# Seven products of a two-layer block in another order, with layer-two blocks between them, four buffers for early heads, weight conversions queued behind them, and one subtraction on VectorE

## The chip, the core and the metric

The kernel runs on one core of a Trainium2 chip. The core has a matrix engine (TensorE, PE in the profile; its weight loads are PEld), three engines for elementwise work (VectorE or DVE, ScalarE or ACT, GpSimd or POOL), and a queue (SyncE, SP) that issues every DMA here. Each engine works its own queue in order; semaphores hold an instruction until what it reads is written and what it overwrites has been read. The metric is device time in microseconds; less is better.

## The reference

Windowed attention with a linear position bias, then a two-layer block with a piecewise-quadratic gate:

```python
# q, k, v: 8 batches x 8 heads x 576 tokens x 64, f32 (q and k times 8)
scores = scale * q @ k.T - slope[h] * abs(i - j)
scores = where((i - j >= 0) & (i - j < 128), scores, -1e9)
attn = exp(scores - max) / (sum + 1e-9)
x = (attn @ v), heads side by side          # 4608 tokens x 512
h = x @ w_in                                # 512 x 2048
g = where(h >= 1, h, where(h <= -1, 0, (h + 1)**2 / 4))
out = g @ w_out                             # 2048 x 512
```

Inputs are drawn at random; `w_in` and `w_out` reach the chip as 64-bit floats.

## The kernel before

**Tiling.** The 36 blocks of 128 tokens form ten chunks (`SIZES`, L54): 2 blocks, eight times 4, and 2. Chunk c is worked in two steps: its attention (8 heads, in four pairs) fills `xn[c]`, the transposed activations; then a *sweep* over the 16 column groups of the hidden layer takes them through both layers. While the sweep of chunk c runs, the attention of chunk c+1 is emitted between its steps (`emit_attention`, L478; the attention's pieces stand in the list `segments`, L458, and run an eighth of a sweep ahead). A scheduler puts each engine's instructions in order from the program's order, taken as priority, and from a simulated time line.

**Precision.** From chunk 2 on a f32 operand is split in two parts, a rounded one and the rest, as fast `fp32r` numbers, and a product is made of two or three fast matmuls. Chunks below `LIGHT = 2` (L62) use plain f32 matmuls in the attention instead (one matmul, two instructions of the engine, no split). So `prepare_q` (L232), `prepare_k` (L252) and `prepare_v` (L263) make split copies only from chunk 2 on.

**One head.** `scores` (L273): PE writes scores, VectorE folds the window into one 128x128 tile per block (L302, L304), ScalarE takes the exponential (L306), the row sums are inverted (L308, L309) and scale `z`, on VectorE in light chunks (L311), on ScalarE otherwise (L314). `weights_t` (L316), a head later: PE transposes `z` (L323), ScalarE copies the result to `lu` (L326), VectorE makes its rest (L328), and GpSimd makes two triangular halves of it (L336, L338) for the two key blocks that a query block sees. `values` (L341), two heads later: PE multiplies by v (L363), and the result goes to `xn` (L366 in light chunks; L368 and L369 otherwise). `lu` has one buffer, `z` two. In the light chunks a matmul of `values` covers up to two query blocks.

**First sweep.** `first_sweep` (L587) takes plain f32 weights. They are made on the chip from the 64-bit words: `fetch_raw` (L127) loads a 0.5 MB tile into one of six buffers, and `convert` (L132) takes two ScalarE and two VectorE operations (L140, L143, L144, L147). There are 32 tiles; `weights_upto` (L485) emits conversions during the attention of chunk 0 and during the first sweep.

**The other sweeps.** A group g of a full sweep has seven products (`PRODUCTS`, L29), a Strassen-like scheme in which 2x2 quarters of weights (A11 ... S4) meet quarters of tokens (B11 ... T4). Each product is six fast matmuls of 256 columns (L411), into one of two accumulator banks, `hA` and `hB`. In `prod` (L533) the bank of product n is A for n = 0, 2, 3, 4 and B for 1, 5, 6. Products 2, 3 and 4 go on accumulating onto what A holds, so ScalarE takes a snapshot first (L539), and VectorE adds snapshots to results of B (L542, L547, L549). L544 copies the last state of A. Each finished tile `h` goes through `nonlinear` (L416): VectorE clamps (L418), ScalarE squares (L419), VectorE takes the maximum (L424), ScalarE rounds it to `gh` (L430), and GpSimd subtracts to make the rest `gl` (L431).

**Layer two.** `layer2` (L434) is a block of three fast matmuls of 512 columns (L445 to L447) from `gh` and `gl` into one of four accumulators. The eight blocks of group g are emitted between the products of group g+1 (`later`, L519): 1, 1, 2, 1, 1, 2 after products 1 to 6. The eight blocks of the last group go into the next sweep, one after each step.

**Weights and tokens.** In sweep 1 `build` (L170) splits each weight quarter and stores it to DRAM; later sweeps fetch it, ten ahead (`AHEAD`, L506), into a ring of ten buffers. `tokens_ready` (L391) lists, by product number, which token quarters of the next chunk may be split (`split_x`, L382) or combined (`combine`, L388) during the last group of a sweep, once the old quarter in the same buffer has had its last use. T2 is made after B22 has been split and overwritten.

Of the kernel before, what the change touches and what calls it, by code (L numbers as in the profile page):

```python
# [28 lines left out]
PRODUCTS = (("A11", "B11"), ("A12", "B21"), ("S2", "T2"), ("S1", "T1"), ("S4", "B22"), ("S3", "T3"), ("A22", "T4"))  # L29
# [5 lines left out]
def windowed_attention_then_ffn(  # L35
# [26 lines left out]
    LIGHT = 2  # L62
# [14 lines left out]
    def bank(c, name):  # L77
        turn[0] += 1
        if c < LIGHT and turn[0] % 2:
            return ps_acc.tile([P, 4 * P], F32, name=name, tag="acc1")  # L80
        return ps_a.tile([P, 4 * P], F32, name=name, tag="ps_a")
# [104 lines left out]
    pair, head, xn = {}, {}, {}  # L186
# [86 lines left out]
    def scores(m, blks):  # L273
# [4 lines left out]
        if m not in head:  # L278
            head[m] = dict(z=ap.tile([P, 4, P], F32, name=f"z_{m}", tag="z", bufs=2),
                           nmax=ap.tile([P, 4], F32, name=f"nmax_{m}", tag="nmax", bufs=2),  # L280
                           sum=ap.tile([P, 4], F32, name=f"sum_{m}", tag="sum", bufs=2),
                           rc=ap.tile([P, 4], F32, name=f"rc_{m}", tag="rc", bufs=2))
# [24 lines left out]
        if blks[-1] == nb - 1:  # L307
            V.tensor_scalar(rc[:, :nb], sm[:, :nb], 1.0e-9, None, ALU.add)  # L308
            V.reciprocal(rc[:, :nb], rc[:, :nb])  # L309
            if c < LIGHT:  # L310
                V.tensor_tensor(z[:, :nb], z[:, :nb], rc[:, :nb].unsqueeze(2).broadcast_to([P, nb, P]), ALU.mult)  # L311
# [4 lines left out]
    def weights_t(m):  # L316
# [3 lines left out]
        lu = head[m]["lu"] = ap.tile([P, 2, 8, P], F32R, name=f"lu_{m}", tag="lu")  # L320
# [3 lines left out]
        ns = 1 if c < LIGHT else 2  # L324
        kind = F32 if c < LIGHT else F32R
        S.copy(lu[:, 0, 1:2 * nb:2].bitcast(kind), pt)  # L326
        if ns == 2:
            V.tensor_tensor(lu[:, 1, 1:2 * nb:2], pt, lu[:, 0, 1:2 * nb:2].bitcast(F32), ALU.subtract)  # L328
        if ns == 2 and nb < 4:
            flat = lu[:, :, :2 * nb]  # L330
            odd, even, n = [flat[:, s, 1::2] for s in range(2)], [flat[:, s, 0::2] for s in range(2)], nb
        else:
            flat = lu.rearrange("p s i w -> p (s i) w")[:, :2 * nb * ns]
            odd, even, n = [flat[:, 1::2]], [flat[:, 0::2]], nb * ns
        for a, b in zip(odd, even):
            G.affine_select(out=b.bitcast(kind), in_=a.bitcast(F32), pattern=[[0, n], [-1, P]],  # L336
                            base=0, channel_multiplier=1, compare_op=ALU.is_gt, fill=0.0)
            G.affine_select(out=a.bitcast(kind), in_=a.bitcast(F32), pattern=[[0, n], [1, P]],  # L338
                            base=0, channel_multiplier=-1, compare_op=ALU.is_ge, fill=0.0)

    def values(m):  # L341
# [13 lines left out]
        todo = [(i, s) for i in range(first, nb) for s in range(1 if c < LIGHT else 2)]  # L355
# [346 lines left out]
```

## Time and profile before

| what | us |
|---|---|
| median of three runs (lowest, highest) | 1143.41 (1140.61, 1147.15) |
| the profiled execution | 1146.27 |
| its span, first to last instruction | 1144.2 |
| first row of the output issued, sweep of chunk 0 | 150.7 |
| the same for chunk 1 | 301.3 |
| the same for chunk 7 | 999.5 |
| last row of the output issued | 1140.1 |

The profile is of one execution. Rows of the views have the line of the kernel, the engine, the operation, the tile written and the tiles read, a count, the busy time in us and the mean in ns of one; behind the second bar stands the idle time of the engine just before them and what ended it. Matmuls overlap in the pipeline, so PE's busy time says less than the distance between the starts of its matmuls. The granted clock is the share of TensorE's full clock.

### The profile page before, as it was taken

Reading aid. Unit: us, or ns where it says so; the run is one execution under the profiler, and the core shown is the slowest. Engines: PE = TensorE matmul, PEld = TensorE weight load, DVE = VectorE, ACT = ScalarE, POOL = GpSimd, SP = SyncE. Lnnn points to the kernel's source line nnn. Section 1 sums busy time; section 2 is a strip of 40 time slices with the busy share of each in tenths; the row PEclk is TensorE's granted clock in tenths of the full one; section 3 lists DMA queues with packets and bytes.
Section 4 is the critical chain, followed back from the end, with each engine's and each line's share of the span. In section 5 each row is a group of like instructions: output and inputs, shape, how many; then the busy total and the mean of one; then the engine's idle time right before and its main releaser. Section 6 shows DMA issues by size and latency. Waiting matters only on the chain.

```text
span 1144.2 us, 19669 instructions
## 1 busy us (share of the span) xinstructions
PE 1046.4 (91%) x6320; PEld 919.0 (80%) x6320; DVE 802.8 (70%) x1934; ACT 744.7 (65%) x1894; POOL 404.7 (35%) x370
## 2 busy tenths in 40 slices
PE   5689978799899999998999899989999989999998
PEld 4567767688788878887989798868888879888897
DVE  6796579899777786777767866775669866864232
ACT  6895368677776676666767666755667765665332
POOL 3211135463333344333434243423333433433222
PEclk7699979999999999998999899989999999999999
DMA  9862135445666566656656666645565745565562
GB/s 327 303 230 67 45 109 172 158 150 179 207 183 186 159 203 181 183 157 190 180 167 191 176 179 182 175 140 170 175 175 177 208 151 169 154 198 155 169 202 74
DMA packets 102342, 199.01 MB, mean 174 GB/s; under 512 B 11361, under 2 KB 14945, under 8 KB 102241
## 3 DMA queue, kind: packets, MB, share of 16 engines
q1 hardware_dynamic: 102240, 197.77, 56.8%
q8 instruction: 51, 0.84, 0.3%
q14 instruction: 51, 0.41, 0.1%
HBM read 171.51 MB, written 26.21 MB: 173 GB/s over the span
## 4 chain that ended last, share of the span: by engine, by line
PE 67%; DVE 15%; ACT 10%; issue 4%; DMA 2%; POOL 1%; SPq 1%; DVEq 0%; ACTq 0%; POOLq 0%
PE hA L411 12%; PE acc L445 10%; PE acc L446 10%; PE acc L447 9%; PE hB L411 8%; PE x L363 5%; PE acc L442 2%; PE p L323 2%; PE h L596 2%; PE h L411 2%; PE s L299 2%; ACT m L419 2%; DVE ql L250 2%; PE s L300 2%; DVE h L424 1%
## 5 line engine op out<-in xcount | busy, mean ns | idle before, releaser
L431 POOL TENSOR_TENSOR gl<-h,gh 128x512 fp32r<-128x512 f32 x128 | 192.1, 1507 | 263.8 <-ACT gh L430 251.2
L445 PE MATMUL acc<-wo,gh 128*128 128x512 f32 x544 | 218.3, 401 | 5.6 <-ACT gh L430 5.6
L336 POOL TENSOR_SCALAR_AFFINE_SELECT lu<-lu 128x1024 fp32r<-128x1024 f32 (+3 forms) x88 | 85.2, 968 | 379.6 <-DVE lu L328 248.3
L446 PE MATMUL acc<-wo,gh 128*128 128x512 f32 x544 | 215.7, 397 | 0.0
L447 PE MATMUL acc<-wo,gl 128*128 128x512 f32 x544 | 163.3, 399 | 0.0
L306 ACT ACTIVATE z<-z,nmax 128x128 f32<-128x128 f32 x288 | 113.5, 395 | 58.8 <-DVE nmax L304 57.7
L419 ACT ACTIVATE m<-m,half 128x512 f32<-128x512 f32 (+1 forms) x160 | 107.8, 679 | 56.7 <-DVE m L418 53.3
L418 DVE TENSOR_SCALAR m<-h 128x512 f32<-128x512 f32 (+1 forms) x160 | 72.3, 458 | 78.6 <-ACT h L544 54.0
L445 PEld LDWEIGHTS acc<-wo,gh 128*128 128x128 f32 x544 | 104.1, 191 | 27.6 <-ACT gh L430 7.9
L424 DVE TENSOR_TENSOR h<-h,m 128x512 f32<-128x512 f32 x128 | 115.1, 903 | 14.5 <-ACT m L419 14.3
L446 PEld LDWEIGHTS acc<-wo,gh 128*128 128x128 f32 x544 | 104.2, 192 | 19.2
L411 PE MATMUL hA<-x_T,w_S 128*128 128x256 f32 x672 | 104.0, 289 | 14.3 <-ACT s L539 12.5
L411 PEld LDWEIGHTS hA<-x_T,w_S 128*128 128x128 f32 x672 | 91.9, 191 | 23.5 <-ACT s L539 16.9
L314 ACT ACTIVATE z<-z,rc 128x128 f32<-128x128 f32 x240 | 77.9, 392 | 50.3 <-DVE rc L309 49.7
L447 PEld LDWEIGHTS acc<-wo,gl 128*128 128x128 f32 x544 | 94.9, 190 | 12.7 <-POOL gl L431 0.2
L302 DVE COPY_PREDICATED s<-older,s 128x256 f32<-128x256 uint32 x144 | 60.8, 422 | 61.5 <-PE s L300 46.9
L539 ACT COPY s<-hA 128x256 f32<-128x256 f32 x192 | 69.7, 363 | 48.0 <-PE hA L411 47.4
L430 ACT CAST gh<-h 128x512 fp32r<-128x512 f32 x128 | 79.2, 621 | 25.3 <-DVE h L424 25.0
L363 PEld LDWEIGHTS x<-lu,vs 128*128 128x128 f32 x608 | 83.7, 192 | 12.3 <-POOL lu L338 4.8
L363 PE MATMUL x<-lu,vs 128*128 128x128 f32 (+1 forms) x608 | 84.8, 275 | 6.4 <-POOL lu L338 3.9
L338 POOL TENSOR_SCALAR_AFFINE_SELECT lu<-lu 128x1024 fp32r<-128x1024 f32 (+3 forms) x88 | 88.2, 1002 | 4.9 <-DVE lu L328 1.1
L323 PE MATMUL p<-ident,z 128*128 128x128 f32 x288 | 58.1, 292 | 19.9 <-ACT z L314 9.0
(116 smaller groups left out, 2217.9 us busy)
## 6 DMA issues: line engine op xcount, KB each, us to landing
w_S<-d_S SPq DMA_DIRECT2D x224, 256.0 KB, 3.0
w_A<-d_A SPq DMA_DIRECT2D x200, 256.0 KB, 2.8
kr<-in_k_dram SPq DMA_DIRECT2D x61, 320.0 KB, 4.9
vn<-in_v_dram SPq DMA_DIRECT2D x32, 320.0 KB, 3.5
out_dram<-o SPq DMA_DIRECT2D x36, 256.0 KB, 2.7
qr<-in_q_dram SPq DMA_DIRECT2D x33, 256.0 KB, 4.7
raw<-in_moe_w_in_dram SPq DMA_DIRECT2D x16, 512.0 KB, 5.5
raw<-in_moe_w_out_dram SPq DMA_DIRECT2D x16, 512.0 KB, 5.1
```

Source lines behind the costliest of these rows:

```text
L306: S.activation(z[:, i], z[:, i], AF.Exp, bias=nmax[:, i:i + 1], scale=-1.0, accum_out=sm[:, i:i + 1])
L323: T.transpose(pt[:, i], z[:, i], ident)
L336: G.affine_select(out=b.bitcast(kind), in_=a.bitcast(F32), pattern=[[0, n], [-1, P]], base=0, channel_multiplier=1, compare_op=ALU.is_gt, ...
L338: G.affine_select(out=a.bitcast(kind), in_=a.bitcast(F32), pattern=[[0, n], [1, P]], base=0, channel_multiplier=-1, compare_op=ALU.is_ge, ...
L363: T.matmul(px[:, q0 * P:q1 * P], st, mv.rearrange("p a w -> p (a w)"), start=(w == 0), stop=(w == len(todo) - 1), skip_group_check=True)
L411: T.matmul(o, w[:, a, kb], x[:, b, kb], start=start and n == 0, stop=stop and n == len(todo) - 1, skip_group_check=True)
L419: S.activation(m, m, AF.Square, bias=half[:, 0:1], scale=0.5)
L424: V.tensor_tensor(f, h, m, ALU.max)
L431: G.tensor_tensor(gl, f, gh.bitcast(F32), ALU.subtract)
L445: T.matmul(a, gh[:, ts], w[:, 0], start=first, stop=False)
L446: T.matmul(a, gh[:, ts], w[:, 1], start=False, stop=False)
L447: T.matmul(a, gl[:, ts], w[:, 0], start=False, stop=last)
```

## The change

- **Order of the products.** (S3, T3) moves from place 5 to place 3; (S1, T1) and (S4, B22) move one back. The banks become A B A B A A B, the snapshots are taken after products 0, 2 and 4, and the sum with B's first part (L547 before) is made after product 4. The token quarters become ready in the new order: T3 after product 3, T1 after 4, B22 and T2 after 5.
- **Urgent evacuation.** Snapshots, sums and the copy of A are emitted at a priority 200 places ahead.
- **Layer two.** Blocks go through one list `waiting` for all sweeps; `second` emits the oldest, and only while more than four are left. Places: 2, 0, 2, 2, 1, 1 after products 1 to 6.
- **gl on VectorE** instead of GpSimd (L431).
- **LIGHT = 3.** Chunk 2's attention is plain f32 as well. The alternate use of an accumulator bank for attention stays with chunks 0 and 1 (`FIRST = 2`).
- **Light heads.** The two triangular halves become two tiles, `own` and `old`; a matmul of `values` covers one query block, and each pair of query and key block has its own.
- **Early heads.** For chunk 0 `z` and the two halves take buffers of later tiles, four each; `weights_t` comes two heads and `values` three heads behind `scores` for chunk 0 (one and two as before from chunk 1 on).
- **Conversions behind.** Eight conversions are emitted during chunk 0's attention, each queued behind a head's copy and scaling on the same engines; the others come two for each step of the first sweep, queued behind its square and maximum, and the first ten builds behind its last four steps.

```diff
-PRODUCTS = (("A11", "B11"), ("A12", "B21"), ("S2", "T2"), ("S1", "T1"), ("S4", "B22"), ("S3", "T3"), ("A22", "T4"))
+PRODUCTS = (("A11", "B11"), ("A12", "B21"), ("S2", "T2"), ("S3", "T3"), ("S1", "T1"), ("S4", "B22"), ("A22", "T4"))
...
-    LIGHT = 2
+    LIGHT = 3
+    FIRST = 2
...
-            head[m] = dict(z=ap.tile([P, 4, P], F32, name=f"z_{m}", tag="z", bufs=2),
+            head[m] = dict(z=fp.tile([P, 2, P], F32, name=f"z_{m}", tag="sw", bufs=4) if c == 0 else
+                           ap.tile([P, 4, P], F32, name=f"z_{m}", tag="z", bufs=2),
...
+        if c < LIGHT:
+            if c < FIRST:
+                own, old = [fp.tile([P, 4, P], F32, name=f"{x}_{m}", tag=x, bufs=4)[:, :nb] for x in ("gh", "gl")]
+            else:
+                both = ap.tile([P, 2, 8, P], F32, name=f"lu_{m}", tag="lu")
+                own, old = both[:, 0, :nb], both[:, 1, :nb]
+            head[m]["lu"] = own, old
+            copied = S.copy(own, pt)
+            G.affine_select(out=old, in_=own, pattern=[[0, nb], [-1, P]],
+                            base=0, channel_multiplier=1, compare_op=ALU.is_gt, fill=0.0)
+            G.affine_select(out=own, in_=own, pattern=[[0, nb], [1, P]],
+                            base=0, channel_multiplier=-1, compare_op=ALU.is_ge, fill=0.0)
+            turned[m] = [copied.ins, head[m]["scaled"].ins]
+            return
...
-        todo = [(i, s) for i in range(first, nb) for s in range(1 if c < LIGHT else 2)]
+        todo = [(i, s) for i in range(first, nb) for s in range(2)]
+        if c < LIGHT:
+            todo = [(i, s) for i, s in todo if 0 <= i + s < nb]
...
-            4: [lambda: split_x(c, "B22", "B22"),
+            3: [lambda: split_x(c, "T3", "B12")],
+            4: [lambda: split_x(c, "T1", "B11")],
+            5: [lambda: split_x(c, "B22", "B22"),
                 lambda: combine(c, "B22", "B22", "B11"),
                 lambda: split_x(c, "T2", "B22"),
-                lambda: split_x(c, "T1", "B11"),
                 lambda: combine(c, "B21", "B21", "B22")],
-            5: [lambda: split_x(c, "T3", "B12")],
...
-        G.tensor_tensor(gl, f, gh.bitcast(F32), ALU.subtract)
+        V.tensor_tensor(gl, f, gh.bitcast(F32), ALU.subtract)
...
+        d1, d2 = (2, 3) if m < H else (1, 2)
+        work.append((m + d2, 0, m, [lambda m=m: values(m)]))
+        work.append((m + d1, 2, m, [lambda m=m: weights_t(m)]))
...
+    def behind(instructions, f):
+        with ExitStack() as stack:
+            for i in instructions:
+                stack.enter_context(tc.issue_after(i))
+            f()
...
-                    o = st["A" if n in (0, 2, 3, 4) else "B"]
-                    product(o, use(c, g, w), xs[c, x], start=n in (0, 1, 5), stop=True)
-                    if n in (0, 2, 3):
-                        s = st[n] = fp.tile([P, 2 * P], F32, name=f"s{n}_{c}_{g}", tag=f"s{n}", bufs=1)
-                        S.copy(s, o)
+                    o = st["A" if n in (0, 2, 4, 5) else "B"]
                     f1, f2 = st["h"]
-                    if n == 1:
-                        V.tensor_tensor(f1[:, :2 * P], o, st[0], ALU.add)
-                    if n == 4:
-                        S.copy(f1[:, 2 * P:], o)
+                    product(o, use(c, g, w), xs[c, x], start=n in (0, 1, 3), stop=True)
+                    with tc.high_priority(offset=URGENT):
+                        if n in (0, 2, 4):
+                            s = st[n] = fp.tile([P, 2 * P], F32, name=f"s{n}_{c}_{g}", tag=f"s{n}", bufs=1)
+                            S.copy(s, o)
+                        if n == 1:
+                            V.tensor_tensor(f1[:, :2 * P], o, st[0], ALU.add)
+                        if n == 4:
+                            V.tensor_tensor(f2[:, 2 * P:], st["B"], st[4], ALU.add)
+                        if n == 5:
+                            S.copy(f1[:, 2 * P:], o)
+                        if n == 6:
+                            V.tensor_tensor(f2[:, :2 * P], o, st[2], ALU.add)
+                    if n == 5:
                         nonlinear(c, g, f1, 4 * P)
...
-                for n, fill in ((2, 1), (3, 2), (4, 1), (5, 1), (6, 2)):
+                for n, fill in ((1, 2), (2, 0), (3, 2), (4, 2), (5, 1), (6, 1)):
...
+    KEEP = 4
+
+    def second():
+        if len(waiting) > KEEP:
+            waiting.pop(0)()
...
+                    weights_upto(EARLY + 2 * n + 2, squared[fc])
+                    if n >= NFC - 4:
+                        behind(squared[fc], lambda: operands_upto(3 * (n - NFC + 4) + 1))
...
+    EARLY = 8
+    while at[0] < ready[1]:
+        emit_attention(at[0] + 1)
+        if turned and converted[0] < EARLY:
+            last = max(turned)
+            if last + 1 > converted[0]:
+                weights_upto(converted[0] + 1, turned[last])
+    weights_upto(EARLY, turned[H - 1])
```

More of the change, by code (lines that the diff above doesn't have):

```diff
@@ L78, in bank @@
         turn[0] += 1
-        if c < LIGHT and turn[0] % 2:
+        if c < FIRST and turn[0] % 2:
             return ps_acc.tile([P, 4 * P], F32, name=name, tag="acc1")
@@ L182, in fetch @@
         return t
-    pair, head, xn = {}, {}, {}
+    pair, head, xn, turned = {}, {}, {}, {}
     lo_rows = [slice(0, D), slice(D, P)]
@@ new lines, in weights_t @@
+        lu = head[m]["lu"] = ap.tile([P, 2, 8, P], F32R, name=f"lu_{m}", tag="lu")
+        S.copy(lu[:, 0, 1:2 * nb:2], pt)
+        V.tensor_tensor(lu[:, 1, 1:2 * nb:2], pt, lu[:, 0, 1:2 * nb:2].bitcast(F32), ALU.subtract)
+        if nb < 4:
+            odd, even, n = [lu[:, s, 1:2 * nb:2] for s in range(2)], [lu[:, s, 0:2 * nb:2] for s in range(2)], nb
+        else:
+            flat = lu.rearrange("p s i w -> p (s i) w")
+            odd, even, n = [flat[:, 1::2]], [flat[:, 0::2]], 2 * nb
@@ L418, in nonlinear @@
         V.tensor_scalar(m, h, 1.0, -1.0, ALU.min, ALU.max)
-        S.activation(m, m, AF.Square, bias=half[:, 0:1], scale=0.5)
+        a = S.activation(m, m, AF.Square, bias=half[:, 0:1], scale=0.5)
         if SIZES[c] == 2:
@@ L516, in sweep_steps @@
     def sweep_steps(c):
-        steps, before = [], []
-        def later(k):
-            take, before[:] = before[:k], before[k:]
-            return take
+        steps = []
         for g in range(NG):
@@ L561, in sweep_steps @@
                 steps.append([begin, lambda prod=prod: prod(0), lambda tokens=tokens: tokens(0)])
-                steps.append([lambda prod=prod: prod(1), lambda tokens=tokens: tokens(1)])
-                steps += [[f] for f in later(1)]
-                for n, fill in ((2, 1), (3, 2), (4, 1), (5, 1), (6, 2)):
+                for n, fill in ((1, 2), (2, 0), (3, 2), (4, 2), (5, 1), (6, 1)):
                     steps.append([lambda prod=prod, n=n: prod(n), lambda tokens=tokens, n=n: tokens(n)])
-                    steps += [[f] for f in later(fill)]
+                    steps += [[second]] * fill
             else:
@@ L574, in plain @@
                     nonlinear(c, i * NG + g, h, 2 * P)
-                steps.append([lambda plain=plain: plain(0)])
-                steps += [[f] for f in later(2)]
-                steps.append([lambda plain=plain: plain(1)])
-                steps += [[f] for f in later(2)]
+                for i in range(2):
+                    steps.append([lambda plain=plain, i=i: plain(i)])
+                    steps += [[second]] * 2
             for i in range(2):
@@ L612, in windowed_attention_then_ffn @@
         load_qk(p)
[L613 to L617 removed]
+        load_v(p)
     keep_busy(16)
@@ L663, in windowed_attention_then_ffn @@
             operands_upto(AHEAD)
-    for f in pending:
-        f()
+    KEEP = 0
+    while waiting:
+        second()
 _INS = ["q", "k", "v", "moe_w_in", "moe_w_out"]
```

117 lines of the change are left out of this document (39 added, 78 removed).

## The prediction

> **What bounds the kernel now.** I read the page first, for the engines' shares, and then the view that gives busy time by stretch, cut where the work changes: heads of the first chunk, first sweep, second sweep (c = 1), six even sweeps (c = 2 to 7), sweep 8, sweep 9.
>
> ```profile
> span 1144.2 us, 19669 instructions
> PE 1046.4 (91%) x6320; PEld 919.0 (80%) x6320; DVE 802.8 (70%) x1934; ACT 744.7 (65%) x1894; POOL 404.7 (35%) x370
> ```
>
> ```profile
> 0.00:63.00 63.00, 37.90 (x134) 29.97 (x135) 44.89 (x138) 45.85 (x116) 18.40 (x42) 0.70 0.90 314
> 63.00:147.00 84.00, 81.69 (x354) 60.62 (x353) 55.63 (x175) 48.67 (x130) 12.11 (x17) 1.00 0.32 95
> 147.00:300.00 153.00, 128.62 (x755) 112.88 (x754) 135.73 (x292) 113.41 (x297) 70.68 (x59) 0.91 0.51 160
> 300.00:999.00 699.00, 660.62 (x4219) 592.18 (x4218) 506.61 (x1179) 472.25 (x1201) 261.30 (x196) 0.98 0.60 177
> 999.00:1099.00 100.00, 97.35 (x623) 87.68 (x622) 46.98 (x123) 51.03 (x124) 32.69 (x43) 1.00 0.59 176
> ```
>
> The columns after the length are PE, PEld, DVE, ACT, POOL, granted clock, DMA share, GB/s. Four regimes show: a start in which no engine is full, a first sweep in which PE is (81.7 of 84), a second sweep that VectorE nearly fills (135.7 of 153), and even sweeps where PE looks full. How full PE really is there, the timeline tells by start times:
>
> ```profile
> 507.61 0.40 PE L446 MATMUL acc<-wo,gh 128*128 128x512 f32 x1
> 507.85 0.87 PE L411 MATMUL hB<-x_T,w_S 128*128 128x256 f32 x6
> 508.55 0.88 PE L411 MATMUL hA<-x_T,w_S 128*128 128x256 f32 x6
> ```
>
> Unstalled, a 512-column matmul takes 0.23 us and six of 256 columns 0.70, 0.117 each. An even sweep has 336 of the latter in products (39.3), 192 of the former in layer2 (44.2), and 8 heads at an estimated 2.3: 14 at 0.117, 4 half as wide, 4 transposes in the 0.44 shown below. That is 102; six make 612 of 699. So 87 us are lost, 14 a sweep. What PE's weight loads waited for, from 300 to 1100 (first four and last of 15 rows, 57 us in all):
>
> ```profile
> PEld hA L411 <- ACT s L539: 21.2, 27, 2.1
> PEld p L323 <- ACT z L314: 8.1, 13, 1.4
> PEld acc L445 <- ACT gh L430: 7.2, 10, 1.3
> PEld hB L411 <- DVE h L542: 4.7, 4, 2.2
> PEld hB L411 <- DVE h L547: 3.7, 5, 1.1
> ```
>
> ```profile
> PEld acc L447 <- POOL gl L431: 0.2, 1, 0.2
> ```
>
> The bank that a product accumulates into must first be copied out: that is the largest wait. The last row matters as well: nobody waits for gl on GpSimd.
>
> **Product order, urgent evacuation, deeper lag.** Before, the banks go A B A A A B B; after, A B A B A A B. Two of three snapshots (L539) now have a product of the other bank, 0.70 us, between copy and reuse; the third has two layer2 blocks, 2 x 3 x 0.23 = 1.4. The blocks come from a list that keeps four, so gh is older when used. The rows for s, h (L542, L547) and gh make 37 of 57 us; of the 87 lost that is 56. I take three quarters, **42**, since every copy still queues behind other work of ACT and DVE; bounds 0 and 75 (nearly all of 87). Urgency moves short copies ahead of attention work, which is emitted an eighth of a sweep early; without that cover its price is the z row, 8.1, once more. Four gh and gl buffers still do: at most four tiles are alive. In sweep 8 the same edits give 3, in sweep 9 about 1: **4**.
>
> **gl on VectorE.**
>
> ```profile
> L431 POOL TENSOR_TENSOR gl<-h,gh 128x512 fp32r<-128x512 f32 x128 | 192.1, 1507 | 263.8 <-ACT gh L430 251.2 <-PE p L323 12.2
> L338 POOL TENSOR_SCALAR_AFFINE_SELECT lu<-lu 128x1024 fp32r<-128x1024 f32 x56 | 70.7, 1262 | 2.1
> L424 DVE TENSOR_TENSOR h<-h,m x128: 660/692/1815, 172.7 to 1090.8; 128x512 f32<-128x512 f32 x128
> L424 DVE TENSOR_TENSOR h<-h,m 128x512 f32<-128x512 f32 x128 | 115.1, 903 | 14.5 <-ACT m L419 14.3
> ```
>
> The subtraction has L424's shape, so 0.69 each on DVE: 16 a sweep are 11.0, and 96 in the even sweeps 66. Against that, L424 has a median of 692 ns, a mean of 903 and a longest of 1815; in the timeline the long ones lie beside GpSimd work. The excess is 0.21 x 96 = 20 us in six sweeps, and the other DVE operations on two SBUF tiles together have, I estimate, as much. gl is 96 x 1.5 = 144 of GpSimd's 261, 55%, so 22 of 40 go. DVE: 507 + 66 - 22 = 551, of 657 us if the forecast holds: 84%, not full. I put this edit at nothing on the path; the remaining quarter above is its cover. Bounds: a gain of 22, or a loss of 44 where DVE sets the pace.
>
> The Trainium skill, page SBUF — State Buffer, section Who interferes with whom, says that VectorE and GpSimd share a pair of SBUF ports as a lock held for a whole instruction, which a VectorE operation with two SBUF inputs takes against a GpSimd one that reads SBUF. The spread of L424 agrees. It speaks against this edit in part: gl now has two SBUF inputs on VectorE, and meets the affine selects that stay. With those busy 117 of 699 us, and half of 1.26 us to wait, that estimate is 16 x 0.17 x 0.63 = 1.7 us a sweep, and the 42 would be 32.
>
> **Chunk 2 without the split (LIGHT = 3).** It lies in the second sweep, where DVE is the limit.
>
> ```profile
> L261 DVE TENSOR_TENSOR kl<-kr,kk 128x1280 fp32r<-128x1280 f32 x28 | 46.7, 1669 | 2.6 <-ACT kk L260 2.6
> L271 DVE TENSOR_TENSOR vs<-vn,vs 128x640 fp32r<-128x640 f32 x28 | 23.6, 842 | 1.4 <-ACT vs L270 0.5
> L250 DVE SCALAR_TENSOR_TENSOR ql<-qr,ql 64x512 fp32r<-64x512 f32 x56 | 52.9, 945 | 1.8
> L328 DVE TENSOR_TENSOR lu<-p,lu 128x512 fp32r<-128x512 f32 x56 | 38.3, 683 | 5.5 <-ACT lu L326 5.4
> L369 DVE TENSOR_TENSOR xn<-x,xn 64x512 f32<-64x512 f32 x56 | 38.0, 679 | 39.3 <-ACT xn L368 38.8
> L311 DVE TENSOR_TENSOR z<-z,rc 128x512 f32<-128x512 f32 x8 | 5.5, 690 | 0.2
> ```
>
> Removed per pair of heads: 1.67 + 0.84 + 2 x 0.95 + 2 x 0.68 + 2 x 0.68 = 7.1; added, two scalings and one copy at 0.69: 2.1. Four pairs: 20 us of DVE gone. ACT loses its casts and scalings too. DVE there: 135.7 - 20 + 11 (gl) - 6 (collisions) = 121. PE pays:
>
> ```profile
> 89.24 0.44 PE p L323 x4
> 89.67 0.87 PE s L297 x4
> 90.54 1.73 PE h L596 x8
> 92.27 1.72 PE acc L442 x4
> ```
>
> A plain f32 matmul of 256 columns is two instructions of 0.216, against two at 0.117 for the split: scores 1.73 instead of 0.94 a head; values, now 8 matmuls of 128 columns, 16 instructions of an estimated 0.12, 1.9 instead of 0.94. That is 14 us for chunk 2, and 1.5 for chunk 1 (16 instructions instead of ten). PE there: 102 + 14 = 116, DVE 121. The even sweeps take 699/612 = 1.14 of their floor; with less waiting I take 1.12 of 117: 131 instead of 153, **22** saved. Bounds: 10 and 33.
>
> **Start: four buffers, conversions behind.** VectorE's first work on scores, and the values of head 0 and of head 7, the last of the first chunk:
>
> ```profile
> 6.47 0.43 DVE L302 COPY_PREDICATED s<-older,s 128x256 f32<-128x256 uint32 x1 [2.70 <-PE s L297]
> ```
>
> ```profile
> 17.44 1.65 PE L363 MATMUL x<-lu,vn 128*128 128x256 f32 x4 [1.22 <-POOL lu L338]
> ```
>
> ```profile
> 61.56 0.92 PE L363 MATMUL x<-lu,vn 128*128 128x256 f32 x4 [0.55 <-POOL lu L338]
> ```
>
> A head takes 44.1/7 = 6.3 us, by latency: one lu buffer. ACT's 45.9 in these 63 us hold 21 conversions (first row, L140 alone in that stretch):
>
> ```profile
> 0.00:63.00 63.00, 13.99 (x21) 0.70 0.90 314
> L140 ACT ACTIVATE raw<-raw 128x512 f32<-128x512 f32 x32 | 21.4, 669 | 2.3 <-DMA raw<-in_moe_w_in_dram 2.3
> L144 DVE TENSOR_SCALAR w<-raw 128x512 int32<-128x512 int32 x32 | 15.1, 471 | 3.0 <-ACT raw L140 2.8
> L147 DVE CUSTOM_DVE_ANT_0 w<-raw,w 128x1024 uint16<-128x1024 uint16 x32 | 23.2, 726 | 1.7
> ```
>
> Each costs ACT two operations, 1.33, and DVE 1.2. With 8 instead of 21 and the builds' casts later, ACT has about 27 us and DVE 24. From the first scores at 6.5 that ends at 33.5; the last head's chain, about one head's 6.3, makes 40 instead of 62. The new wait: ACT's exps queue behind a conversion whose raw tile is in flight. The one such wait cost 2.3; eight would be 18, and I keep 3: 43 instead of 63, where the stretch was cut. SP issues the raw fetches later with them: 24 x 0.52 MB over some 90 us is 140 GB/s, where the start moved 314.
>
> The first sweep's PE floor stays: 16 x 1.73 (h), 32 x 0.43 x 2 (acc), 8 heads at 3.9 (scores 1.73, values by their columns the same, transposes 0.44), some 86, of which a little runs early; 84 were taken. It now holds 13 more conversions and ten builds: DVE 55.6 + 16 + 6 = 78. I add 6 for that. It ends at 43 + 84 + 6 = 133 instead of 147: **14** saved; bounds 0 and 20.
>
> **Sum.** 14 + 22 + 42 + 4 = 82. The span goes from 1144.2 to 1062; the profiled execution was 1146.27, so 1064; it stood 2.9 above the median of 1143.41, so **1061** on that scale.
>
> **Rivals.**
> VectorE takes over: with gl in its queue, copies and nonlinear steps come late as often as now. For it: 25.4 of 28 us DVE busy where one sweep meets the next (504 to 532); against it: those are the stretched operations. Start 10, second sweep 14, even sweeps 0: 1143 - 24 = 1119. The Trainium skill, Perfetto Trace Analysis, Optimizing Scalar/DVE Operations, warns that moving work between GpSimd and VectorE might not help, since they share a port; that is this rival.
>
> ```profile
> L385 ACT CAST x_T<-xn 128x512 fp32r<-128x512 f32 x32 | 19.7, 618 | 16.5 <-DVE xn L389 16.1
> 504.00:532.00 28.00, 24.38 (x139) 21.19 (x139) 25.39 (x49) 17.56 (x43) 12.30 (x8) 0.94 0.50 148
> ```
>
> Stalls vanish: PE is fed, and its clock never drops. Start 18, second sweep 33, even sweeps 75, sweep 8 and 9 together 7: 1010.
>
> Slower: tokens for T2 are now split only after (S4, B22), the sixth product of a sweep, and needed at the third product of the next. PE's cover is three products and four blocks, 3 x 0.7 + 4 x 0.69 = 4.9; the chain is two casts at 0.62 and three DVE operations at 0.69, 3.3, or 5.5 when stretched, with an estimated 4 us of nonlinear work (twice max and gl at 0.69, and the smaller steps) in the same queue. If that misses by 9 at each of 7 boundaries and order gains nothing else, 1143 - 36 + 63 = 1170. From 5.1 us a boundary the whole is slower.
>
> Nothing shows: the scheduled queues already hid the copies, and the later conversions hold the first sweep as long as they held the heads: about 1140.
>
> **Chances.** Forecast (1030 to 1095) 0.61, VectorE 0.15, stalls vanish 0.12, slower 0.07, nothing 0.05. The range 1010 to 1122 leaves out half of the second-best case, a little of VectorE's and the last two. Faster by over 0.5% (about what a measurement here can tell) 0.88, same 0.05, slower 0.07.
>
> **What would show it.** Values of head 7 near 42; first sweep done near 133; second sweep's DVE near 121; waits for s under 8 us; L424's mean under 800 ns; even sweeps near 109. Wrong if the third product of a sweep waits for T2, if ACT waits for raw tiles, or if DVE is over 90% busy in the even sweeps.

## The result, and the profile after

Four runs of the changed kernel have a median of 1098.8 us (1089.9 to 1102.9), those of the kernel before beside them 1144.0. The ratio is 0.9595, 95% interval [0.9522, 0.9668]: faster by 4%, where 1061 us, 7%, had been forecast; the time lies in the range of 1010 to 1122. The profiled execution, at 1102.9 us the slowest of the four, compares with 1146.3 of the one before.

The page of the changed kernel begins:

```profile
span 1101.2 us, 19641 instructions
PE 1037.2 (94%) x6432; PEld 914.3 (83%) x6432; DVE 810.6 (74%) x2058; ACT 724.4 (66%) x1850; POOL 202.2 (18%) x226
```

GpSimd has half its work left (405 before), and VectorE only 8 us more than before although it took over the subtraction; in the second sweep it has 19 us less (135.7 before). The view of busy time by stretch, cut where the work changes, with the columns of the prediction's view (length, PE, PEld, DVE, ACT, POOL, granted clock, DMA share, GB/s):

```profile
0.00:43.00 43.00, 32.96 (x179) 27.70 (x180) 30.68 (x125) 30.81 (x92) 15.07 (x40) 0.92 0.81 278
43.00:120.00 77.00, 75.81 (x355) 56.68 (x354) 63.33 (x178) 61.58 (x151) 13.63 (x18) 1.00 0.59 196
120.00:258.00 138.00, 129.24 (x820) 115.36 (x819) 116.91 (x297) 94.56 (x256) 36.27 (x42) 0.99 0.53 174
258.00:961.00 703.00, 664.39 (x4238) 593.74 (x4237) 525.07 (x1280) 475.00 (x1207) 124.51 (x102) 0.98 0.60 177
961.00:1057.00 96.00, 95.15 (x608) 85.58 (x607) 56.38 (x139) 48.93 (x120) 12.72 (x24) 1.00 0.57 175
```

The first stretch shrank from 63 to 43 us, the first sweep from 84 to 77, the second from 153 to 138. The six even sweeps did not shrink: 703 us beside 699. Cut at the first output DMA of each chunk, as in the table of the profile before, the two profiled executions stand so:

| stage | before | after | difference | forecast |
|---|---|---|---|---|
| start and first sweep | 150.7 | 125.4 | -25.3 | -14 |
| second sweep | 150.6 | 133.1 | -17.5 | -22 |
| six even sweeps (c = 2 to 7) | 698.2 | 702.8 | +4.6 | -42 |
| sweeps 8 and 9 | 140.2 | 135.7 | -4.5 | -4 |

(The rest, before the first and behind the last of these marks, makes up the 43.4 us between the two executions.) Everything that was won lies outside the stretch in which most had been expected. What PE's weight loads waited for there, first in the kernel before (301 to 999 us, four of its 14 rows, which sum to 53.6 us), then in the changed one (258 to 961, seven of its ten rows, which sum to 57.7); columns are the total in us, the number of waits, and the longest:

```profile
PEld hA L411 <- ACT s L539: 19.0, 24, 2.1
...
PEld acc L445 <- ACT gh L430: 6.7, 9, 1.3
PEld hB L411 <- DVE h L542: 4.7, 4, 2.2
PEld hB L411 <- DVE h L547: 3.7, 5, 1.1
```

```profile
PEld hB L427 <- DVE h L569: 14.8, 13, 3.4
PEld hA L427 <- ACT s L561: 14.3, 24, 1.6
PEld acc L462 <- ACT gh L447: 7.3, 10, 1.1
PEld p L324 <- ACT z L316: 6.1, 9, 1.3
PEld hB L427 <- DVE h L563: 5.2, 6, 0.9
PEld hB L427 <- DVE h L565: 3.4, 5, 0.8
PEld hA L427 <- ACT h L567: 2.9, 7, 0.4
```

The wait for the snapshots (s) fell by 5 us. The wait for a sum out of bank B (h) rose from 4.7 + 3.7 = 8.4 to 14.8 + 5.2 + 3.4 = 23.4, and the one for gh stayed. The largest row is new: L569 is the last sum of a group, L549 before, for which none of the 14 rows of before stands.

### The profile page after: what moved, and what is told of

It reads as the page before. It is cut to its first block, busy times and chain, and to the rows that moved or that the text cites. A ratio compares the mean times of both kernels' runs of the same rounds, so it can differ in the third digit from the quotient of the medians.

```text
span 1101.2 us, 19641 instructions
## 1 busy us (share of the span) xinstructions
PE 1037.2 (94%) x6432; PEld 914.3 (83%) x6432; DVE 810.6 (74%) x2058; ACT 724.4 (66%) x1850; POOL 202.2 (18%) x226
## 4 chain that ended last, share of the span: by engine, by line
PE 71%; DVE 14%; ACT 8%; issue 4%; DMA 2%; SPq 0%; POOL 0%; DVEq 0%; ACTq 0%; POOLq 0%
PE hA L427 12%; PE acc L462 11%; PE acc L463 10%; PE acc L464 9%; PE hB L427 9%; PE x L379 5%; PE acc L459 2%; PE h L623 2%; PE p L324 2%; PE h L427 2%; PE s L299 2%; PE s L301 2%; DVE ql L251 2%; PE s L302 2%; DVE m L434 2%
## 5 line engine op out<-in xcount | busy, mean ns | idle before, releaser
L462 PE MATMUL acc<-wo,gh 128*128 128x512 f32 x544 | 221.6, 407 | 9.1 <-ACT gh L447 8.6
L463 PE MATMUL acc<-wo,gh 128*128 128x512 f32 x544 | 217.9, 401 | 0.0
L348 POOL TENSOR_SCALAR_AFFINE_SELECT lu<-lu 128x1024 fp32r<-128x1024 f32 (+1 forms) x64 | 69.6, 1088 | 631.1 <-DVE lu L341 572.5
L464 PE MATMUL acc<-wo,gl 128*128 128x512 f32 x544 | 166.9, 396 | 0.3 <-DVE gl L448 0.2
L434 DVE TENSOR_SCALAR m<-h 128x512 f32<-128x512 f32 (+1 forms) x160 | 78.8, 500 | 55.8 <-ACT h L567 42.4
L440 DVE TENSOR_TENSOR h<-h,m 128x512 f32<-128x512 f32 x128 | 97.2, 765 | 5.8 <-ACT m L435 5.0
L448 DVE TENSOR_TENSOR gl<-h,gh 128x512 fp32r<-128x512 f32 x128 | 96.8, 765 | 3.5 <-ACT gh L447 2.8
L304 DVE COPY_PREDICATED s<-older,s 128x256 f32<-128x256 uint32 x144 | 60.6, 421 | 43.0 <-PE s L302 33.5
L447 ACT CAST gh<-h 128x512 fp32r<-128x512 f32 x128 | 78.0, 618 | 16.4 <-DVE h L440 16.1
L316 ACT ACTIVATE z<-z,rc 128x128 f32<-128x128 f32 x208 | 67.3, 391 | 24.0 <-DVE rc L311 23.4
L379 PEld LDWEIGHTS x<-lu,vs 128*128 128x128 f32 x528 | 71.5, 190 | 3.5 <-POOL lu L348 0.5
L306 DVE CUSTOM_DVE_ANT_0 z<-s,rel 128x128 f32<-128x128 f32 x288 | 71.7, 284 | 2.3
L379 PE MATMUL x<-lu,vs 128*128 128x256 f32 (+1 forms) x528 | 72.7, 272 | 0.3 <-POOL lu L348 0.3
L350 POOL TENSOR_SCALAR_AFFINE_SELECT lu<-lu 128x1024 fp32r<-128x1024 f32 (+1 forms) x64 | 70.2, 1097 | 6.5 <-DVE lu L341 2.4
```

Of the source, the lines that this page charges most:

```text
L306: V.tensor_tensor_reduce(out=z[:, i], in0=pt[:, n, P:], in1=distances(b0 + i), op0=ALU.add, op1=ALU.min, scale=-slope, scalar=3.0e38, accu ...
L379: T.matmul(px[:, q0 * P:q1 * P], st, mv.rearrange("p a w -> p (a w)"), start=(w == 0), stop=(w == len(todo) - 1), skip_group_check=True)
L434: V.tensor_scalar(m, h, 1.0, -1.0, ALU.min, ALU.max)
L440: b = V.tensor_tensor(f, h, m, ALU.max)
L447: S.copy(gh, f)
L448: V.tensor_tensor(gl, f, gh.bitcast(F32), ALU.subtract)
```

## The experiments

Theory V: the order, the urgency and the lag pay in the even sweeps, and something else in the change (gl on VectorE) takes their gain back. Theory O: they gain nothing there, because the bank waits only move to other copies. Expectations from the second group on name further theories, each with what it means in its place. Later experiments ask what the even sweeps are made of. Kernels are the changed one with one edit, unless something else is said. A stage's time is from the one profiled execution of each; ratios are to the kernel before.

### gl back on GpSimd; the old order

```diff
-        V.tensor_tensor(gl, f, gh.bitcast(F32), ALU.subtract)
+        G.tensor_tensor(gl, f, gh.bitcast(F32), ALU.subtract)
```

> The changed kernel with one line undone: gl is subtracted on GpSimd again. Theory V (VectorE's new work gave back what the order of the products won in the even sweeps): the even sweeps fall from 117 to about 110 us each, the whole to 1050-1070. Theory O (the order itself won nothing, and gl on VectorE is neutral or a help because GpSimd no longer collides with VectorE): the maximum's mean rises from 0.77 back to about 0.9 us, the whole is 1095-1130.

1113.3 us, ratio 0.9741 [0.9719, 0.9763]: 14 us slower than the change. The second sweep is 5.5 us longer and sweep 8 5.7. The even sweeps take 702.9 us, as with gl on VectorE, but at a granted clock of 0.99 where the profiled execution of the change had 0.98, and with 65.2 us of waits of PE's weight loads instead of 57.7. Theory V falls with this: gl on VectorE took nothing away. Two groups of VectorE work in the even sweeps (busy us, mean ns), first of this kernel, then of the changed one:

```profile
L440 DVE TENSOR_TENSOR h<-h,m 128x512 f32<-128x512 f32 x96 | 88.6, 927 | 1.0 <-ACT m L435 0.8
L251 DVE SCALAR_TENSOR_TENSOR ql<-qr,ql 64x512 fp32r<-64x512 f32 x44 | 49.2, 1118 | 1.4
```

```profile
L440 DVE TENSOR_TENSOR h<-h,m 128x512 f32<-128x512 f32 x96 | 74.1, 778 | 5.1 <-ACT m L435 4.6
L448 DVE TENSOR_TENSOR gl<-h,gh 128x512 fp32r<-128x512 f32 x96 | 72.6, 768 | 2.7 <-ACT gh L447 2.4
...
L251 DVE SCALAR_TENSOR_TENSOR ql<-qr,ql 64x512 fp32r<-64x512 f32 x44 | 30.2, 686 | 1.4
```

With gl on GpSimd these VectorE operations stretch: 149 ns on each maximum, 432 on each `ql`. PE's waits move too: for L569 they fall from 14.8 us to 0.7, for gh (L447) they rise from 7.3 to 21.3.

```diff
-PRODUCTS = (..., ("S2", "T2"), ("S3", "T3"), ("S1", "T1"), ("S4", "B22"), ("A22", "T4"))
+PRODUCTS = (..., ("S2", "T2"), ("S1", "T1"), ("S4", "B22"), ("S3", "T3"), ("A22", "T4"))
...
-                    o = st["A" if n in (0, 2, 4, 5) else "B"]
+                    o = st["A" if n in (0, 2, 3, 4) else "B"]
...
-                for n, fill in ((1, 2), (2, 0), (3, 2), (4, 2), (5, 1), (6, 1)):
+                for n, fill in ((1, 1), (2, 1), (3, 2), (4, 1), (5, 1), (6, 2)):
...
```

(With it go the snapshots, sums and token steps at their old places.)

> The changed kernel with the old order of the seven products, the old places of the layer-two blocks and the old times of the tokens; the list that keeps four, the urgent copies, gl on VectorE, the light chunk and the start stay. Theory V: the order is worth some 40 us, so this is 1130-1145. Theory O: 1085-1110, even sweeps 115-118 as in both kernels.

1103.1 us, 0.9656 [0.9620, 0.9692]; even sweeps 699.7. In this kernel the two blocks behind the last product share one list (`[[second]] * 2`), so that the step appended to it in the second sweep, the split of layer two's weights, is issued twice for each group. The second time it splits the rest that the first time left, so the large, rounded part of those weights is left out of the computation. It was run again without that.

### The old order with steps of their own; the lag

```diff
-                    steps += [[second]] * fill
+                    steps += [[second] for _ in range(fill)]
```

> order_old with each group's layer-two weights split once, as they should be. Theory C (the even sweeps are paced by what stands before the copies in the queues of ScalarE and VectorE, not by which bank comes next): 1090-1105, even sweeps as in the changed kernel (697-705 us for six). Theory B (the new order does win bank waits, and something else in this list loses them): 1110-1130, even sweeps 710-730.

1116.1 us, 0.9749 [0.9710, 0.9788]; even sweeps 711.0, second sweep 137.4. By itself this says that the new order is worth 17 us, 8 of them in the even sweeps. But this kernel and the last differ only in 16 splits of the second sweep, and stand 13 us apart, 11 of them in the even sweeps, where their programs are the same. Those 11 us are the granted clock, 0.98 against 0.99 (last table of this section); PE's waits are 3 us smaller here, 60.8 to 63.9. A difference of some 10 us between two single edits can thus be one between two schedules, with no cause in the edit.

```diff
-    KEEP = 4
+    KEEP = 0
```

> The changed kernel with KEEP = 0: the list of layer-two blocks is emptied as it comes, so the lag is that of before. Theory V and theory O both: if the four kept blocks cover late gh, this is slower by the gh waits, 5-15 us (1105-1115); if they cover nothing, 1090-1103.

1129.0 us, 0.9874 [0.9852, 0.9896]: 30 us slower than the change, more than either expectation, even sweeps 722.1. In the new order the lag is needed. PE's waits for gh do not grow, though (5.4 us in place of 7.3); the largest new ones are those of `values` for `lu` (9.6 and 8.5 us). That fits a PE which, without blocks in reserve, has no other work ready when attention comes late.

### The kernel before with gl on VectorE

```diff
-        G.tensor_tensor(gl, f, gh.bitcast(F32), ALU.subtract)
+        V.tensor_tensor(gl, f, gh.bitcast(F32), ALU.subtract)
```

> The kernel before with one line changed: gl on VectorE. Theory V: VectorE has 66 us more in the even sweeps and they lose some 40 us: 1175-1190. Theory O: VectorE's gain from fewer collisions pays for it: 1130-1150.

1136.1 us, 0.9943 [0.9923, 0.9964]: some 7 us faster than before, from the second sweep (142.5, not 150.6); even sweeps 699.1. So the edit helps in both kernels.

### No urgency; LIGHT = 2; a third output buffer

```diff
-    URGENT = 200
+    URGENT = 0
```

> The changed kernel with the copies out of the banks at ordinary priority. Theory C: they queue behind more attention work and the even sweeps lose 10-30 us: 1110-1130. Theory B, or if the urgent copies only push the attention and nonlinear work back: 1085-1105.

1094.9 us, 0.9563 [0.9531, 0.9596]: not to be told from the change. Even sweeps 695.8; PE's waits for s are 14.3 us, 24 times, as with the urgency. The copies run where they ran. The stretch that follows shows how; first ACT, then PE, in the timeline of the changed kernel (start, us, line, operation, in brackets the idle time before it and what ended it):

```profile
436.35 1.27 ACT L261 CAST kk<-kr 128x1280 fp32r<-128x1280 f32 x1 [0.58 <-PE s L301]
437.52 0.72 ACT L435 ACTIVATE m<-m,half 128x512 f32<-128x512 f32 x1
438.15 1.26 ACT L250 ACTIVATE ql<-qr 64x512 fp32r<-64x512 f32 x2
439.44 0.72 ACT L435 ACTIVATE m<-m,half 128x512 f32<-128x512 f32 x1
440.07 0.35 ACT L561 COPY s<-hA 128x256 f32<-128x256 f32 x1
```

```profile
436.27 0.88 PE L427 MATMUL hA<-x_B,w_A 128*128 128x256 f32 x6
436.99 0.88 PE L427 MATMUL hB<-x_B,w_A 128*128 128x256 f32 x6
437.71 1.35 PE L379 MATMUL x<-lu,vs 128*128 128x128 f32 x10
440.47 0.98 PE L427 MATMUL hA<-x_T,w_S 128*128 128x256 f32 x6 [1.41 <-ACT s L561]
```

Bank A was full by 437.2. Its snapshot ran at 440.07, 2.9 us later, behind a cast, two squares and two scalings of q that are not urgent, and PE, which had a product of bank B and ten matmuls of `values` to do in between, stood 1.41 us. So the higher priority did not bring the snapshot to the head of the queue. It changed the order of almost nothing: compared by line, operation and tiles, 16 of ScalarE's 1850 instructions, 8 of VectorE's 2058, 100 of PE's 6432 and none of GpSimd's stand at another place in the two traces. The 7 us between the even sweeps of these two kernels are then not the edit's; they are the granted clock. Why the scheduler moved so little the runs don't show.

```diff
-    LIGHT = 3
+    LIGHT = 2
```

> The changed kernel with LIGHT = 2: chunk 2's attention is split again. Both theories: the second sweep (133 us) gets its 20 us of VectorE work back and loses the 14 us of TensorE work; if VectorE sets its pace, 143-150 and the whole 1108-1118; if TensorE does, 120-130 and the whole below 1095. The even sweeps stay.

1119.2 us, 0.9778 [0.9742, 0.9813]: chunk 2 without the split is worth 20 us, but 2 of them in the second sweep (135.0, not 133.1). The first even sweep behind it takes 133.9 us, not 117.5. The 15 us from the border of these sweeps, by stretch, first with LIGHT = 2, then in the change, and PE's longest wait of that sweep with LIGHT = 2:

```profile
260.00:275.00 15.00, 8.59 (x40) 7.49 (x40) 13.76 (x28) 10.17 (x26) 2.52 (x2) 0.68 0.59 165
```

```profile
258.00:273.00 15.00, 14.54 (x99) 13.02 (x98) 11.77 (x33) 10.96 (x32) 4.37 (x4) 1.00 0.78 244
```

```profile
PEld hA L427 <- DVE x_T L402: 2.7, 1, 2.7
```

With the split, VectorE carries its backlog over the border (13.76 of 15 us busy), the tokens come late, PE gets 40 matmuls out where the other kernel gets 99, and its granted clock falls to 0.68.

```diff
-            o = fp.tile([P, DM], F32, name=f"o_{c}_{t}", tag="o")
+            o = fp.tile([P, DM], F32, name=f"o_{c}_{t}", tag="o", bufs=3)
```

This goes at the longest wait for L569. First VectorE, then PE in the timeline of the changed kernel, where sweep 3 ends:

```profile
499.00 0.69 DVE L467 COPY o<-acc 128x512 f32<-128x512 f32 x1 [1.96 <-DMA out_dram<-o]
499.72 0.42 DVE L569 TENSOR_TENSOR h<-hB,s 128x256 f32<-128x256 f32 x1
```

```profile
500.20 0.98 PE L427 MATMUL hB<-x_B,w_A 128*128 128x256 f32 x6 [3.21 <-DVE h L569]
```

An output copy waits for its buffer, the sum queues behind it, and PE for the sum.

> The changed kernel with three buffers for the output tile instead of two. In the changed kernel VectorE and ScalarE stand still at the end of a sweep until an output DMA has left a buffer, and a product's copy waits behind (3.2 us of TensorE at 497-500). Theory C: 1.5-3 us less at each of 8 ends, 1075-1090. Theory B: that wait is hidden anyway, 1093-1103.

1099.8 us, 0.9604 [0.9563, 0.9644]: no change. The longest wait for L569 is now 2.1 us, but its sum 13.8, against 14.8: others came in its place.

### All three undone

Old order (with steps of their own), URGENT = 0 and KEEP = 0 together, the rest of the change as it is.

> The changed kernel with three parts undone at once: the old order and places, no urgency, no blocks kept. The start, the light chunk and gl on VectorE stay. The prediction's step (order, urgency and lag win 42 us in the six even sweeps): they rise to 735-745, the whole to 1135-1145. Theory N (the three together win nothing against what was there before): six even sweeps 695-710, the whole 1090-1108.

1106.9 us, 0.9684 [0.9658, 0.9711]. Even sweeps and PE's waits in them (two of 13 rows; all of them 55.2 us from 261 to 954):

```profile
261.00:954.00 693.00, 653.70 (x4217) 586.80 (x4215) 527.10 (x1278) 472.00 (x1201) 132.55 (x102) 0.99 0.61 178
```

```profile
PEld hA L427 <- ACT s L561: 23.0, 33, 2.1
PEld hB L427 <- DVE h L563: 11.5, 8, 2.0
```

Undoing all three costs 8 us by the medians, and none of it in the even sweeps: 692.9, where the change has 702.8 (the difference is the clock, 0.99 against 0.98). It lies in the second sweep (+4.1), sweep 8 (+5.7) and sweep 9 (+1.5). The waits for s are larger by 9 us and those for L569 smaller by 11 (4.1); the sum of all is 55.2 against 57.7. Theory N holds: the three edits moved the waits.

### Less work for one engine at a time

Each of these leaves work out, to see what paces the even sweeps: the first the product of the rest `gl` with the weights in layer two, the second that rest itself (its matmul reads `gh` instead), the third the division by the row sums from chunk 3 on.

```diff
             T.matmul(a, gh[:, ts], w[:, 0], start=first, stop=False)
-            T.matmul(a, gh[:, ts], w[:, 1], start=False, stop=False)
-            T.matmul(a, gl[:, ts], w[:, 0], start=False, stop=last)
+            T.matmul(a, gh[:, ts], w[:, 1], start=False, stop=last)
```

> The changed kernel without the third matmul of a layer-two block: TensorE has 64 x 0.23 = 14.7 us less in an even sweep, VectorE and ScalarE have the same work. Left out: the product of gl with the weights. Theory P (TensorE's own work sets the pace, waits ride on top): six even sweeps fall by 75-90, to 613-628. Theory Q (ScalarE's and VectorE's queues set it): by less than 35, to 668-700.

```diff
-        V.tensor_tensor(gl, f, gh.bitcast(F32), ALU.subtract)
-        gs[c, fc] = (gh, gl)
+        gs[c, fc] = (gh, gh)
```

> The changed kernel without the subtraction that makes gl; the third matmul reads gh. VectorE has 16 x 0.69 = 11 us less in an even sweep, TensorE the same work. Left out: gl. Theory P: six even sweeps fall by 0-15. Theory Q: by 30-66.

```diff
-                for i in range(nb):
-                    S.activation(z[:, i], z[:, i], AF.Copy, scale=rc[:, i:i + 1])
+                pass
```

> The changed kernel without the four scalings of a head on ScalarE from chunk 3 on: 32 x 0.39 = 12.5 us less of ScalarE in an even sweep. Left out: the division by the row sums there. Theory P: six even sweeps fall by 0-15 (TensorE also waits less for the transposes). Theory Q: by 30-75.

1009.4 us, 1145.5 us and 1085.6 us; 0.8829 [0.8802, 0.8857], 1.0022 [1.0000, 1.0043], 0.9495 [0.9468, 0.9522]. The even sweeps of the three, by stretch:

```profile
240.00:883.00 643.00, 580.15 (x3835) 524.87 (x3834) 533.27 (x1281) 473.94 (x1206) 115.25 (x101) 0.97 0.65 193
```

```profile
262.00:997.00 735.00, 668.90 (x4214) 594.62 (x4214) 477.85 (x1172) 473.81 (x1197) 111.08 (x100) 0.97 0.59 169
```

```profile
262.00:943.00 681.00, 651.80 (x4217) 583.25 (x4216) 514.32 (x1273) 419.20 (x1008) 120.32 (x100) 0.99 0.61 181
```

Of 88 us of matmuls taken away (384 of 0.23 us) the even sweeps give back 60. Of 56 us of ScalarE's busy time (475 less 419), 22. And 47 us of VectorE's time taken away (525 less 478) make them 32 us longer. Each of the three lies outside what both of its theories had named. In the kernel without the subtraction PE's waits (two of eight rows) are led by:

```profile
PEld acc L460 <- ACT gh L446: 38.0, 29, 3.0
PEld hA L427 <- ACT s L559: 23.3, 17, 1.8
```

The wait for gh was 7.3 us. With the subtraction gone, the scheduler puts blocks of layer two at other places. Counted in the order of PE's instructions in the traces (six even sweeps, all groups but the first of each; a matmul of layer two is a third of a block), the mean number of blocks behind the first to the seventh product that runs is

| kernel | 0 | 1 | 2 | 3 | 4 | 5 | 6 |
|---|---|---|---|---|---|---|---|
| the program of the kernel before | 0 | 1 | 1 | 2 | 1 | 1 | 2 |
| the kernel before, as run | 0.13 | 0.44 | 1.77 | 0.67 | 3.97 | 0.61 | 0.41 |
| the program of the change | 0 | 2 | 0 | 2 | 2 | 1 | 1 |
| the change, as run | 0.17 | 0.55 | 0.82 | 1.81 | 3.42 | 0.74 | 0.49 |
| no urgency | 0.17 | 0.55 | 0.82 | 2.03 | 3.20 | 0.74 | 0.49 |
| KEEP = 0 | 0.07 | 0.53 | 0.93 | 2.02 | 3.53 | 0.67 | 0.25 |
| all three undone | 0 | 0.44 | 1.54 | 1.40 | 4.07 | 0.35 | 0.20 |
| subtraction left out | 0 | 0 | 2.57 | 1.43 | 4.00 | 0 | 0 |

Both programs put four of the eight blocks at places 2 to 4; six or more have gone there in every kernel that was counted, in the kernel before as well (6.4). So products 5, 6, 0 and 1 run with few blocks between them. The products themselves run in another order than the written one, too. This is one group of the kernel before, its third to sixth product, in PE's timeline; by the tiles they are S2, S3, S1 and S4 (S2 and S1 show the same tiles; S2 is the first):

```profile
504.70 0.99 PE L411 MATMUL hA<-x_T,w_S 128*128 128x256 f32 x6 [0.68 <-ACT s L539]
...
507.85 0.87 PE L411 MATMUL hB<-x_T,w_S 128*128 128x256 f32 x6
508.55 0.88 PE L411 MATMUL hA<-x_T,w_S 128*128 128x256 f32 x6
...
514.13 0.87 PE L411 MATMUL hA<-x_B,w_S 128*128 128x256 f32 x6
```

S3, the one product of the three in bank B, is written behind S1 and S4 there. In the 48 groups of the six even sweeps of the kernel before it never runs behind S4; in 37 it runs ahead of both, which is the place that the change writes for it, and in 11 between them. In the change it is 41 and 7. In the kernels with the old order written again it is 43 and 5, 41 and 7 (with steps of their own), and 30 and 18 (all three undone): these undid the written order, and much less the one that runs.

The new wait, the 14.8 us for L569, has several causes, by what VectorE does in the trace between the end of the group's last product and that sum. Of its 13 cases four (8.0 us) come 4 to 7 us behind the end of a sweep, each with an output copy (L467) just ahead, as in the lines above; four (4.5 us) come in the last group of a sweep, behind a clamp (L434) and a token split (L402); three (0.9 us) behind a clamp and a window fold (L304), and two (1.6 us) behind the rests of k and q (L262, L251).

### What the even sweeps are made of

In every trace the granted clock has two values, 1.00 and 0.50. In the even sweeps of the change it is 0.50 in seven stretches of 3.4 or 6.8 us, each of which begins within 5 us of a wait of PE of over 1.1 us. This is the one behind the 3.2 us wait shown above:

```profile
501.40:508.20 6.80, 6.03 (x28) 5.54 (x27) 4.09 (x12) 5.44 (x15) 0.00 (x0) 0.50 0.65 195
```

Half of the time at 0.50 is taken as lost. The length of the six even sweeps, PE's waits in it, what the clock lost, and what is then left, of all fourteen kernels, in us:

| kernel | length | waits | lost to the clock | left |
|---|---|---|---|---|
| less_act | 680.9 | 46.9 | 3.4 | 631 |
| order_old | 699.7 | 63.9 | 5.1 | 631 |
| undo3 | 692.9 | 55.2 | 5.1 | 633 |
| gl_pool | 702.9 | 65.2 | 8.5 | 629 |
| no_urgent | 695.8 | 55.0 | 8.5 | 632 |
| o3 | 699.2 | 58.6 | 10.2 | 630 |
| b_gl_dve | 699.1 | 57.6 | 10.2 | 631 |
| before | 698.2 | 53.6 | 13.7 | 631 |
| after | 702.8 | 57.7 | 15.4 | 630 |
| order_old2 | 711.0 | 60.8 | 17.1 | 633 |
| keep0 | 722.1 | 74.4 | 18.8 | 629 |
| less_dve | 735.1 | 84.0 | 20.5 | 631 |
| light2 | 721.5 | 69.2 | 22.2 | 630 |
| less_pe | 643.0 | 81.1 | 17.1 | 545 |

(The labels are less_act, less_dve and less_pe for the three kernels above, order_old2 for the old order with steps of its own, o3 for the third output buffer, light2 for LIGHT = 2, b_gl_dve for the kernel before with gl on VectorE, gl_pool for the change without it; the others are named by their edit.) In the first thirteen 629 to 633 us are left, whatever the edit: what tells these kernels apart is their waits and the clock. So a sweep of the change is about 630/6 = 105 us of issue at full clock, 3 us of lost clock and 10 of waits. In less_pe the issue fell by 85 us, nearly the 88 that were removed; the waits rose by 23.

## Why the prediction came out as it did

**The sum** was 38 us too low: 42 us that never came, 5 too many in the second sweep, 11 too few in the start; the even sweeps of the profiled execution grew by another 5. The 1098.8 us lie outside the 1030 to 1095 that were given for the forecast's own case, and inside the range only because it was drawn up to 1122 for part of another case. That, and the surplus of the start, is luck: the largest term gave nothing.

**Product order, urgent evacuation, deeper lag: 42, measured none. This is the step that failed**, and it failed twice. First in its size: 87 us were called lost against an estimated floor of 612, and the waits for s, h and gh, 37 of 57 us listed, were scaled up to 56 of those 87. By the last table only 53.6 us were waits. The rest was a floor estimated some 20 us too low (631) and the clock, 14 us. (With 19 + 14 + 54 the 87 are accounted for.) What the waits named could give was at most the 34 in their rows, and what of the 14 hung on them. Second in its mechanism: the argument took the order of products and blocks from the program's text, "the banks go A B A A A B B". PE runs them in the scheduler's order, and in that the kernel before already went A B A B A A B in most groups: S3 stood ahead of S1 and S4 in 37 of 48, and six of the eight blocks ran between S2 and S4 (lines and table above; two of these lines stand in the prediction itself). The cover that the new order was to bring was there, and the blocks ran where the scheduler put them in both kernels. The waits for s were to fall below 8 us and fell to 14.3; those for h rose by 15. The sum of all went from 53.6 to 57.7.

The three steps inside it: the order wrote down what mostly ran already; urgency changed the order of hardly an instruction; the lag, thought of as a help against waits for gh, is worth 30 us in the new order, where the waits that grow without it are those for `lu`. With all three undone the even sweeps are no longer. What they won, 8 us, is in the second sweep and in the last two.

**gl on VectorE: 0, measured a help of 7 (alone) to 14 us (in the change).** The cost was estimated well: 768 ns for each, where 0.69 us had been taken. The relief was not: VectorE is busy 525 us in the even sweeps where it was 507, so of 72.6 us added 54 came back, not the 22 estimated (with that edit alone, in the kernel before, it is 525 beside 506). L424's mean of 960 ns there (903 over all) is 778 as L440, under the 800 named. The Trainium skill, page SBUF — State Buffer, section Who interferes with whom, says that the two engines hold a shared SBUF port in turn; the estimate from it of what gl itself would lose, 10 us in six sweeps, agrees with its excess over the 0.69 us, 96 x 0.08 = 7.5 us. The maximum and `ql` have two SBUF inputs as the rule says, and each maximum over 1.1 times the median ran beside a GpSimd instruction (43 of 43 before, 22 of 22 in the change). The clamp (L434), which reads one tile, is stretched as well, 535 ns on average against a median of 426. What was set free on the other side, seven times as much, was taken too small. The gain lies in the second sweep, in sweep 8, and in the even sweeps' waits (57.7 us against 65.2).

**LIGHT = 3 and the second sweep: 22, measured 17.5**, with VectorE at 116.9 busy of 138 us (121 forecast) and PE at 129 (116 forecast, but as issue time; the 129 are busy time, in which matmuls overlap). The size was near, for a reason that holds in part. With LIGHT = 2 the second sweep is only 2 us longer: what shortened it were other parts, gl on VectorE (5.5 to 8) and the lag (4.6) among those tried. VectorE's relief was worth 20 us, as priced, but it is paid out behind the border, in the sweep that inherits the backlog (133.9 us, not 117.5).

**Start: 14, measured 25.** The mechanism held and two terms were too large. From the timeline of the changed kernel, the end of chunk 0's last head, and the first sweep with its first block of layer two:

```profile
35.08 0.39 PE L379 MATMUL x<-gh,vn 128*128 128x128 f32 x2
...
46.73 1.99 PE L623 MATMUL h<-xn,w 128*128 128x256 f32 x8 [1.19 <-DVE g L440]
48.56 1.88 PE L459 MATMUL acc<-w,g 128*128 128x512 f32 x4
```

Head 7's values are done by 35.5, not 42: that is 2 us behind the 33.5 at which the engines' work had been put, where one head's whole chain (6.3) and 3 us for raw tiles had been added. And the 6 us for conversions in the first sweep were not paid: VectorE, 63 of 77 us, and ScalarE, 62, stay under PE's 76. From 35.7 to 43 PE did attention of chunk 1, which the first sweep then no longer had to hold.

**Sweep 8 and 9: 4, measured 4.5**, and for two reasons where one was given: gl back on GpSimd takes 5.7 of it back, the three edits undone 7.2. The two don't add up; gl on VectorE alone, in the kernel before, shortened sweep 8 by 0.7.

**The rivals.** "VectorE takes over" had the size of the even sweeps right (0) and of the whole nearest (1119), but not why: VectorE is 75% busy there, and taking the subtraction away makes it slower. The new wait is in VectorE's queue, but behind single late instructions, not by its load. The slower one, T2's tokens at the border, has no such wait in the change (PE waits 2.6 us for them in six sweeps); with LIGHT = 2 it shows, once, at 2.7 us.

**Open.** Which part of a difference of some 10 us between two of these kernels belongs to the edit and which to the schedule and the clock that it happened to draw is not settled; the new order's worth between 0 and 17 us is such a case. In the even sweeps of no kernel did S3 run behind S4, so what the old order would cost if it ran as written, and whether the new one would pay in a program whose blocks stay at their written places, was not tried. The best median, 1094.9 us without the urgency, cannot be told from the change.

## What to carry to other kernels

Before pricing an order of work, read the order that ran from the trace of before: a scheduler that reorders makes the program's text a poor witness, and may already have made the move that you are about to price. A wait that is removed may come back at the next copy in the same queue. Take the sum of the rows of the waits, with the clock lost behind them, as the upper bound of what removing them can give, and do not stretch it to the distance from an estimated floor. When VectorE's operations run stretched beside GpSimd's, moving GpSimd's work to VectorE can cost little; read that from the spread of VectorE's durations.

## What the runs showed of the hardware beyond that

- Moving 96 subtractions from GpSimd (1.5 us each) to VectorE (0.77) added 18.5 us to VectorE's busy time, not 72.6: `ql` went from 970 to 686 ns (1118 with gl on GpSimd in the changed kernel), the maximum from 960 to 778.
- A short famine of PE costs more than its length: a wait of 3.2 us was followed by 6.8 us at a granted clock of 0.50. In the 15 us at the sweep border with LIGHT = 2 the clock was 0.68 against 1.00, and over the six even sweeps kernels with 69 us of waits and more lost 17 to 22 us to the clock, those with less 3 to 17.
- Runs of one and the same kernel spread with the clock: the change's four took 1089.9, 1095.0, 1102.6 and 1102.9 us with 0.995, 0.989, 0.980 and 0.980 granted. So a stage's length from one execution is known no better than to some 10 us unless its clock is read with it.
- Less work can be slower: 47 us less of VectorE's time in the even sweeps, 47 us more for the whole.
